# First token pair's FFN steps in two parts, x first in its queue in four parts, four weight blocks decoded ahead of the FFN instead of nine

## The chip, the cores and the metric

The kernel runs on one core of one Trainium2 chip. The metric is the device time of one execution in microseconds (us). The engines are TensorE (PE, its weight loads as PEld), VectorE (DVE), ScalarE (ACT), GpSimd (POOL) and SyncE (SP), which mainly issues DMA transfers. Each engine runs its own instructions in the order in which the program was written down for it.

## The reference

The input x has shape (8, 3008, 256), in fp32. The mixing layer filters each batch along its 3008 positions in the frequency domain, and a feed-forward layer (FFN) with 2048 hidden channels follows:

```python
X = np.fft.rfft(x, axis=1)
Y = X * (filt_r + 1j * filt_i)[None]
y = np.fft.irfft(Y, n=3008, axis=1).astype(np.float32)
t = y.reshape(8 * 3008, 256)
h = t @ w_in                       # 256 -> 2048
g = h * (1.0 / (1.0 + np.exp(-h)))
out = (g @ w_out).astype(np.float32)   # 2048 -> 256
```

The FFN weights `w_in` and `w_out` reach the kernel as 64-bit floats.

## The kernel before

**The transform.** The length 3008 is 47 times 64, and both directions of the transform are matrix products with tables. For a batch the stages are: stage 1 (`pa`, L392 for batch 0, L416 for later ones), a change of layout, `forward` (`pb`, L526), a product with the filter on DVE (`multiply`, L619) and sums (`add`, L627 and L628), `inverse` (`pc`, L660), copies of its result (`rows_first`, L674) that go to DRAM (`d<-q`, L676) and come back in another layout (`load_t4_rows`, L703, to an area of `w_t`), and `stage3` (`pd`, L718), whose result is copied to `y` (L732) as the FFN's operand.

**The head.** Batch 0 is transformed before any FFN work; this stretch is called the head. Its x comes as `x_first` in two transfers of 1536 KB on SP's queue, behind four raw blocks of weights (512 KB each). While PE waits it runs matmuls of no use (`idle`, L1269) on the table `wx_t`. `stage1_first(j)` works on a quarter of the channels each, and DVE transposes its result (L396). The argument `fill` of `forward` sets how many matmuls of no use (L519) stand before it. A later batch's transform is spread over the FFN steps of the batch before it: steps 1 to 6 each take one piece of batch 1's stage 1 (four 512-column matmuls `pa`, L416, and two copies `t<-pa` on ACT, L421).

**The weights.** They come in 16 blocks `j` of raw 64-bit words and are turned into fp32 on the chip. For one block that is: `bits` (two DVE operations, L1170 into `e` and L1172 into `m`), `converted` (two ACT operations on `e`, L1179 and L1180), `added` (DVE, L1186), `signed` (DVE, L1191, needs `converted`), `placed` (DVE, L1198, writes `w_t`). `split` is bits and converted, `rounded` is added and signed. Blocks `2jp` and `2jp+1` hold the weights of the hidden channels of step `jp`, and `combine_weights(jp)` makes three more sums from them (four DVE operations, L948 on `w_t`). The raw words and the intermediate results lie in areas that are free at that time, among them buffers of the pools that the FFN uses later.

**The FFN.** The tokens are in 48 pairs of blocks of up to 256 tokens, six pairs for each batch; each pair takes eight steps (`NJP = 8`), one for each `jp`. A step forms the product of a 2x2 block matrix with seven matrix products instead of eight, in `hidden`, and `project` adds the result through w_out in the same manner one step later (`LAG = 1`). `tokens(pair)` makes the differences of tokens `ty` that `hidden` needs (DVE, L948). In `hidden(step)` (L966) the products go to two PSUM tiles: `px` (A11, then S2, S3 and A22 added on) and `pyz` (A12 in one half, S1 and S4 in the other). Each has one buffer. ACT copies `px` after three of its products (`abc`, L985, L992, L998), DVE adds copies to `pyz` (g0, g2, g1, in this order, L948), ACT applies SiLU (L981), and DVE forms further sums (g4 and g5 in one operation, then g6 and g7). `project(step)` (L1023) makes seven products into four accumulators `acc` (L1044), which stay in PSUM through the eight steps of a pair. After the last step `drain` copies them to a tile `s`, the even ones on ACT and the odd ones on DVE (L1062 and L1064), and POOL makes seven additions on it.

**The order of work.** `hidden` and `project` are generators, and each step has eight rounds. In each round each of the two goes on to its next `yield`; then everything that was put down for that step and round is emitted:

```python
for rnd in range(ROUNDS):
    held = ...
    work = [w for w in work if w in held or next(w, work) is not work]
    until(step + rnd / ROUNDS)
```

`put(step, rnd, piece, *args)` puts a piece of work down, so `(0, 5, (bits, 9), (added, 9))` emits these pieces after round 5 of step 0. In `hidden` g0 is written in round 1, the second copy and the first SiLU in round 2, the third copy and g2 in round 4, and g1 in round 7. The table of decode pieces spreads the blocks that are left after the head over steps 0 to 6. Two more tables, `combines` and `stores`, hold when `tokens(pair)` is emitted and when a pair's result is stored. The head's order is the order of the program's lines.

## Time and profile before

| | |
|---|---|
| median of 3 runs | 2503.47 us (2503.17 to 2504.69) |
| profiled execution | 2503.14 us, its span 2501.4 us |
| granted TensorE clock | 1.00 |
| busy in the span: PE, DVE, ACT, POOL | 2483.7, 1756.4, 1095.6, 430.9 us |
| first product of the FFN begins | 63.06 us |
| pa matmuls of batch 1 in the chain | 71.67, 79.70, 87.74 us |
| PE busy from 63.0 to 111.8 | 48.07 of 48.80 us |
| PE busy from 111.8 to 160.0 | 48.20 of 48.20 us |

Times in the trace count from the span's start. A row of a timeline is: start, duration, engine, line, operation, result and operands with their shapes, number of instructions, and in brackets the idle time before it and what ended that. The mean clock is a share of full speed. The chain of waits is followed back from the last instruction, at each step to what released it.

### The profile page before, as it was taken

How to read it: one execution, taken by the hardware profiler on the slowest of the kernel's cores; microseconds unless marked ns; L12 is line 12 of the kernel's file. 1: busy time of each engine (PE TensorE's matmuls, PEld its weight loads, DVE VectorE, ACT ScalarE, POOL GpSimd, SP SyncE). 2: the span in 40 equal slices, each digit the busy share in tenths (PEclk: the TensorE clock that was granted, in tenths of full speed). 3: DMA queues.
4: the chain of work that ended last, by engine and by line, in shares of the span. 5: the costliest groups of instructions: out<-in, count | busy, mean ns of one | idle time of the engine just before them, and what ended most of it. 6: DMA issues, size and time to landing. Idle time of an engine off the chain costs nothing.

```text
span 2501.4 us, 42281 instructions
## 1 busy us (share of the span) xinstructions
PE 2483.7 (99%) x16242; PEld 2129.1 (85%) x16242; DVE 1756.4 (70%) x3603; ACT 1095.6 (44%) x3006; POOL 430.9 (17%) x673
## 2 busy tenths in 40 slices
PE   8999999999999999999999999999999999999999
PEld 6788888888888888888888888888888888888988
DVE  8866677777777777777777867777677767655544
ACT  4544444444444444444444444444444444444443
POOL 2211112112121122211122112211221111101100
PEclk9999999999999999999999999999999999999999
DMA  8513233213232042420333203321142211200000
GB/s 304 169 60 104 70 72 79 74 38 81 60 93 73 25 93 50 116 63 18 84 74 99 56 26 89 81 68 43 34 107 54 56 43 34 64 21 9 17 9 17
DMA packets 139801, 170.67 MB, mean 68 GB/s; under 512 B 20860, under 2 KB 113372, under 8 KB 138716
## 3 DMA queue, kind: packets, MB, share of 16 engines
q1 hardware_dynamic: 115536, 120.77, 18.2%
q0 software_dynamic: 22080, 44.10, 6.8%
q8 instruction: 127, 2.08, 0.3%
q10 hardware_dynamic: 1984, 3.11, 0.3%
q14 instruction: 74, 0.61, 0.1%
HBM read 96.06 MB, written 81.26 MB: 71 GB/s over the span
## 4 chain that ended last, share of the span: by engine, by line
PE 97%; DMA 1%; DVE 1%; ACT 0%; issue 0%; SPq 0%; POOL 0%; DVEq 0%; ACTq 0%
PE acc L1044 46%; PE px L977 26%; PE pyz L977 20%; PE pd L754 1%; PE pf L486 1%; PE pc L582 1%; PE pb L544 1%; PE pa L392 0%; PE pa L416 0%; DMA w_t<-in_x_first_dram 0%; DMA w_t<-d 0%; DMA d<-q 0%; PE pd L718 0%; PE pb L526 0%; PE pc L640 0%; DVE g L948 0%
## 5 line engine op out<-in xcount | busy, mean ns | idle before, releaser
L1044 PE MATMUL acc<-g,w_t 128*128 128x256 f32 (+1 forms) x5376 | 1507.4, 376 | 3.0 <-ACT o L767 2.5
L1044 PEld LDWEIGHTS acc<-g,w_t 128*128 128x128 f32 x5376 | 1016.2, 190 | 153.8 <-ACT o L767 15.3
L948 DVE TENSOR_TENSOR g<-pyz,abc 128x256 f32<-128x256 f32 (+1 forms) x1152 | 479.7, 416 | 480.3 <-ACT abc L998 240.0
L948 DVE TENSOR_TENSOR g<-g 128x256 f32<-128x256 f32 (+3 forms) x1152 | 589.7, 512 | 196.7 <-ACT g L981 183.6
L977 PE MATMUL px<-ty,w_t 128*128 128x256 f32 (+1 forms) x2304 | 675.6, 375 | 0.6 <-ACT abc L998 0.5
L981 ACT ACTIVATE g<-g 128x256 f32<-128x256 f32 (+1 forms) x1152 | 472.9, 411 | 235.8 <-DVE g L948 235.8
L948 POOL TENSOR_TENSOR s<-s 128x256 f32<-128x256 f32 (+1 forms) x329 | 252.3, 784 | 1419.0 <-DVE s L1062 1093.8
L977 PEld LDWEIGHTS px<-ty,w_t 128*128 128x128 f32 x2304 | 434.1, 190 | 57.2 <-issue 3.7
L977 PE MATMUL pyz<-y,w_t 128*128 128x256 f32 (+1 forms) x1536 | 451.2, 375 | 1.2 <-DVE g L948 1.1
L977 PEld LDWEIGHTS pyz<-y,w_t 128*128 128x128 f32 x1536 | 283.0, 189 | 44.8 <-DVE g L948 5.0
L992 ACT COPY abc<-px 128x256 f32<-128x256 f32 (+1 forms) x384 | 141.4, 368 | 372.7 <-PE px L977 372.7
L981 ACT ACTIVATE g<-px 128x256 f32<-128x256 f32 (+1 forms) x384 | 145.8, 380 | 299.7 <-PE px L977 299.7
L998 ACT COPY abc<-px 128x256 f32<-128x256 f32 (+1 forms) x384 | 141.4, 368 | 308.6 <-PE px L977 308.5
L977 PE MATMUL px<-y,w_t 128*128 128x256 f32 (+1 forms) x768 | 227.4, 378 | 0.1
L977 PE MATMUL pyz<-ty,w_t 128*128 128x256 f32 (+1 forms) x768 | 225.7, 376 | 0.2
L977 PEld LDWEIGHTS px<-y,w_t 128*128 128x128 f32 x768 | 143.4, 189 | 23.7 <-ACT g L981 2.4
L977 PEld LDWEIGHTS pyz<-ty,w_t 128*128 128x128 f32 x768 | 142.0, 190 | 21.9 <-DVE g L948 1.8
L985 ACT COPY abc<-px 128x256 f32<-128x256 f32 (+1 forms) x384 | 135.1, 352 | 34.8 <-PE px L977 34.8
L506 POOL DMA_DIRECT2D d<-tf x96 | 48.5, 506 | 216.3 <-DVE tf L436 210.8
L1062 ACT COPY s<-acc 128x512 f32<-128x512 f32 (+1 forms) x94 | 54.2, 577 | 47.6 <-issue 29.2
L603 POOL DMA_DIRECT2D d<-low x36 | 22.2, 618 | 286.3 <-DVE low L599 286.3
L476 DVE TENSOR_TENSOR uf<-x_all 120x512 f32<-120x512 f32 (+1 forms) x72 | 60.2, 864 | 0.3 <-issue 0.3
(132 smaller groups left out, 1351.5 us busy)
## 6 DMA issues: line engine op xcount, KB each, us to landing
t<-d SPq DMA_DIRECT2D x84, 256.0 KB
t<-d SPq DMA_DIRECT2D x224, 96.0 KB
out_dram<-s SPq DMA_DIRECT2D x64, 256.0 KB
d<-q POOLq DMA_DIRECT2D x48, 256.0 KB, 5.3
x_all<-in_x_dram SPq DMA_DIRECT2D x96, 96.0 KB
x_all<-xr SPq DMA_DIRECT2D x96, 96.0 KB
d<-tf POOLq DMA_DIRECT2D x96, 96.0 KB, 2.7
d<-tq POOLq DMA_DIRECT2D x96, 96.0 KB, 2.9
```

The costliest lines, as they stand in the source:

```text
L476: nc.vector.tensor_tensor(out=out, in0=in0, in1=in1, op=op)
L486: nc.tensor.matmul(out=ps[q][32 * k:32 * k + 32], lhsT=wq_t[rows, k], rhs=rhs[k][rows], start=True, stop=True)
L506: nc.gpsimd.dma_start(out=d1[par, :, grp, at:at + 4], in_=part[rows].rearrange("p q n c -> p (q n) c"))
L544: nc.tensor.matmul(out=ps[k, ri][32 * j:32 * j + 32, a, :], lhsT=dn_t[rows, 4 * (g + a) + at, :], rhs=t2s[g + a][rows, at, :], start=True, ...
L948: eng.tensor_tensor(out=out, in0=in0, in1=in1, op=op)
L977: nc.tensor.matmul(out=out, lhsT=w_t[:, jp, c, 0], rhs=rhs, start=start, stop=True, skip_group_check=True)
L981: nc.scalar.activation(out=g[:, k, 0:n], in_=g[:, k, 0:n] if src is None else src, func=AFT.Silu)
L985: nc.scalar.copy(out=sums[:, 0, 0:n], in_=xo)
L992: nc.scalar.copy(out=sums[:, 1, 0:n], in_=xo)
L998: nc.scalar.copy(out=sums[:, 2, 0:n], in_=xo)
L1044: nc.tensor.matmul(out=acc[pair][i][:, h, 0:n], lhsT=w_t[:, jp, OUT_PLACE.get(c, c), 1], rhs=g[:, k, 0:n], start=(jp == 0 and h == 0), sto ...
L1062: copy(out=s[:, 2 * i:2 * i + 2, 0:n], in_=acc[pair][i][:, :, 0:n])
```

## The change

The steps of pair 0 are done in two parts: its first three (`SPLIT = 3`), then all eight of pair 1, then the other five of pair 0. `drain` therefore runs twice for pair 0, and the second time it adds the accumulators to `s` on DVE. Pair 1's result goes to `x_all`, `tokens(1)` moves from step 7 to step 1, `tokens(2)` from step 11 to step 12 with the tile of `ty[1]`, and the stores of the two pairs change places.

In the head, x comes first in SP's queue, in four transfers of 768 KB, and the raw weights after the tables. The first `idle` runs on a cleared area and so waits for no table; `stage1_first` gets five matmuls of no use before its third and fourth quarter, `forward(0)` gets 12 instead of 8, and the `idle` before stage 3 20 instead of 30.

Before, blocks 0 to 7 were done and 8 nearly done before the FFN. Now blocks 0 to 3 are done, and 4 and 5 as far as `added`. The rest is spread over steps 0 to 9, and raw blocks and intermediate results move to other areas. The diff, cut:

```diff
...
 CH = 256
 STEPS = 2 * len(PAIRS) * NJP
 LAG = 1
+SPLIT = 3
 
 A11, A12, S3, A22, S1, S2, S4 = range(7)
 OUT_PLACE = {A12: S3, S3: A12}
...
 
...
-    return rows.reshape(3, 32, 32, 4, 2, 32).transpose(4, 3, 1, 0, 2, 5)
+    return rows.reshape(3, 32, 32, 4, 4, 16).transpose(4, 3, 1, 0, 2, 5)
 
 
 def laid_out(inputs):
...
 
 
             view = w_t.rearrange("p j c w n -> p (j c w n)")
-            for part in range(2):
-                at = view[:, 3072 * part:3072 * part + 3072]
+            for part in range(4):
+                at = view[:, 1536 * part:1536 * part + 1536]
                 nc.sync.dma_start(out=at, in_=x_first[part].rearrange("q r k n c -> (q r) (k n c)"))
-                xs[part] = at.rearrange("p (k n c) -> p k n c", k=3, c=32)
+                xs[part] = at.rearrange("p (k n c) -> p k n c", k=3, c=16)
...
-        def stage1_first(j):
-
-            ps = [bank(b, f"pa_{b}_{j}_{q}").rearrange("p a c -> p (a c)").rearrange(
-                "p (n c) -> p n c", c=16) for q in range(4)]
-            c0 = 16 * (j % 2)
+        def stage1_first(j, fill=0):
+
+            raw = [bank(b, f"pa_{b}_{j}_{q}") for q in range(4)]
+            ps = [r.rearrange("p a c -> p (a c)").rearrange("p (n c) -> p n c", c=16) for r in raw]
+            for _ in range(fill):
+                nc.tensor.matmul(out=raw[0][:, 0, 0:128], lhsT=wx_t, rhs=wx_t, start=True, stop=True)
             for k in range(3):
                 for q in range(4):
                     rows = slice(32 * q, 32 * q + 32)
-                    nc.tensor.matmul(out=ps[q], lhsT=wx3_t[rows, k], rhs=xs[j // 2][rows, k, :, c0:c0 + 16],
+                    nc.tensor.matmul(out=ps[q], lhsT=wx3_t[rows, k], rhs=xs[j][rows, k],
                                      start=(k == 0), stop=(k == 2), skip_group_check=True)
             for q in range(4):
                 at = 64 * q + 16 * j
...
 
                 view = w_t.rearrange("p j c w n -> p (j c w n)")
                 room = {2: view[:, 1792:3840], 3: view[:, 3840:5888],
-                        5: raws["first"].bitcast(FP32)}[g].rearrange("p (k i r c) -> p k i r c", k=2, i=2, r=2)
+                        5: view[:, 6144:8192]}[g].rearrange("p (k i r c) -> p k i r c", k=2, i=2, r=2)
                 z, pt = room[:, k, 0], room[:, k, 1]
             else:
                 z = zpool.tile([128, 2, C], FP32, name=f"z_{b}_{g}_{k}", tag="z")
...
 
     pairs = token_pairs()
     n_steps = len(pairs) * NJP
+    steps = [divmod(step, NJP) for step in range(n_steps)]
+    steps = [*steps[0:SPLIT], *steps[NJP:2 * NJP], *steps[SPLIT:NJP], *steps[2 * NJP:]]
     v, gp = nc.vector, nc.gpsimd
     ty, g_t, acc, unfinished = {}, {}, {}, []
 
...
     def tokens(pair):
 
...
-        t = typool.tile([128, 4, CH], FP32, name=f"ty_{pair}", tag="ty")
+        t = ty[1] if pair == 2 else typool.tile([128, 4, CH], FP32, name=f"ty_{pair}", tag="ty")
...
-        pair, jp = divmod(step, NJP)
+        pair, jp = steps[step]
...
-        pair, jp = divmod(step, NJP)
+        pair, jp = steps[step]
         n, g = pairs[pair][3], g_t.pop(step)
-        if jp == 0:
+        new = step == 0 or steps[step - 1][0] != pair
+        if new:
             acc[pair] = {}
-        last = jp == NJP - 1
+        last = step == n_steps - 1 or steps[step + 1][0] != pair
 
         order = PROJECT
-        if jp == 0 and step in joined:
+        if new and step in joined:
             order = PROJECT[0:2] + PROJECT[3:5] + PROJECT[2:3] + PROJECT[5:]
             if step in turned:
                 order = order[1::-1] + order[2:]
-        elif jp == 0:
+        elif new:
             order = PROJECT[2:3] + PROJECT[0:2] + PROJECT[3:]
...
-                             start=(jp == 0 and h == 0), stop=last, skip_group_check=True)
+                             start=(new and h == 0), stop=last, skip_group_check=True)
...
-    results = {}
+    results, parts = {}, set()
 
     def drain(pair, i):
         n = pairs[pair][3]
-
-        if i == 0:
+        more = pair == 0 and i in parts
+        if pair == 1:
+            results[pair] = x_all.rearrange("p i a n -> p (i a n)").rearrange("p (k n) -> p k n", n=CH)
+        elif i == 0 and not more:
             results[pair] = spool.tile([128, 8, CH], FP32, name=f"s_{pair}", tag="s")
         s = results[pair]
         copy = v.tensor_copy if i % 2 else nc.scalar.copy
         if i < 3:
-            copy(out=s[:, 2 * i:2 * i + 2, 0:n], in_=acc[pair][i][:, :, 0:n])
+            dst, src = s[:, 2 * i:2 * i + 2, 0:n], acc[pair][i][:, :, 0:n]
+        else:
+            dst, src = s[:, 6, 0:n], acc.pop(pair)[3][:, 0, 0:n]
+        if more:
+            combine(v, dst, src, dst, ALU.add)
+        else:
+            copy(out=dst, in_=src)
+        if pair == 0 and not more:
+            parts.add(i)
             return
-        copy(out=s[:, 6, 0:n], in_=acc.pop(pair)[3][:, 0, 0:n])
+        if i < 3:
+            return
...
-            if j in (6, 7):
-
-                room = w_t.rearrange("p j c w n -> p (j c w n)")[:, (7168, 13056)[j - 6]:][:, 0:1024].bitcast(U32)
-                e, m = room[:, 0:512], room[:, 512:1024]
-            elif j in (0, 1, 4, 5):
+            if j in (0, 1):
                 if "scratch" not in raws:
                     raws["scratch"] = gpool.tile([128, 4, 512], U32, name="scratch", tag="g")
                 e, m = (raws["scratch"][:, 2 * (j % 2) + i] for i in range(2))
...
                 m = ppool.tile([128, 512], U32, name=f"m_{j}", tag="p")
             lo, hi = words[:, :, 0], words[:, :, 1]
             ef, mf = e.bitcast(FP32), m.bitcast(FP32)
-            ends = (lo, hi) if j in (2, 3, 6, 7) else (m, e)
+            ends = (lo, hi) if j in (2, 3, 4, 5) else (m, e)
             raws[j] = lo, hi, e, m, ef, ends[0].bitcast(FP32), ends[1].bitcast(FP32), ends[1]
...
-    def idle(n, ps=None):
-
-        ps = (ps or bank(0, "idle")).rearrange("p a c -> p (a c)")
+    def idle(n, operand=None):
+
+        ps = bank(0, "idle").rearrange("p a c -> p (a c)")
+        rows = wx_t if operand is None else operand
         for _ in range(n):
-            nc.tensor.matmul(out=ps[:, 0:128], lhsT=wx_t, rhs=wx_t, start=True, stop=True)
+            nc.tensor.matmul(out=ps[:, 0:128], lhsT=rows, rhs=rows, start=True, stop=True)
 
...
-    idle(18)
+    blank = x_all[0:96, 0, 0, 0:128]
+    v.memset(blank, 0.0)
+    idle(14, operand=blank)
 
     part, second = spectral(0), spectral(1)
-    weights(0, 1, 2, 3)
     part["load_first"]()
     nc.sync.dma_start(out=d_t[:, 0:16], in_=d_dram[:, 0:16])
     nc.sync.dma_start(out=f_all[:, :, 0:4], in_=filt_a)
...
     nc.sync.dma_start(out=d_t[:, 16:NS], in_=d_dram[:, 16:NS])
     nc.sync.dma_start(out=e_t[:, 2:NG], in_=e_dram[:, 2:NG])
     nc.sync.dma_start(out=wi_t, in_=ws_dram.ap())
-    weights(4, 5, 6, 7)
-    for pair in ((0, 1), (2, 3)):
-        split(*pair)
-        rounded(*pair)
+    weights(0, 1, 2, 3)
 
...
     for j in range(4):
-        part["stage1_first"](j)
+        part["stage1_first"](j, 5 * (j > 1))
     second["load_two"]()
-    weights(8)
-    part["forward"](0, fill=8)
-    placed(0, 1)
+    weights(4, 5)
+    part["forward"](0, fill=12)
     for g in range(1, 4):
         part["forward"](g)
 
...
     for k in range(2):
         part["add"](NG - 1, k)
     part["load_t4_rows"](0)
-    bits(4)
+    bits(0, 1)
     inverse(4)
-    bits(5)
     inverse(5)
-    combine_weights(0)
-    bits(6, 7, 8)
+    converted(0, 1)
+    added(0, 1)
     part["load_t4_rows"](1)
     part["load_t4_rows"](2)
-    converted(4, 5)
-    placed(2, 3)
-    weights(9)
+    bits(2, 3)
+    converted(2, 3)
+    signed(0, 1)
+    placed(0, 1)
     for u in range(2):
         second["stage1"](u, False)
-    converted(6, 7)
-    converted(8)
-    rounded(4, 5)
-    placed(4, 5)
-    rounded(6, 7)
-    placed(6, 7)
-    added(8)
-    signed(8)
-    idle(30)
+    combine_weights(0)
+    rounded(2, 3)
+    placed(2, 3)
+    combine_weights(1)
+    bits(4, 5)
+    converted(4, 5)
+    added(4, 5)
+    idle(20)
     for g in range(4):
         part["stage3"](g)
     gp.tensor_copy(out=gate, in_=y[0, 0][:, 0, 28:29])
...
     idle_wide(1)
     nc.sync.dma_start(out=wi_t, in_=wi_dram.ap())
     second["load_x"](2)
-    weights(10, 11, 12)
+    weights(6, 7)
     second["load_x"](3)
     early[0] = None
     plan_rest(0, part)
     for g in (4, 5):
-        put(7, 0, part["load_t4"], g)
+        put(8, 0, part["load_t4"], g)
     for step, t, dram in ((20, wq_t, wq_dram), (40, dn_flat, dn_dram),
                           (40, en_flat, en_dram), (30, wm_t, wm_dram)):
         put(step, 0, lambda t=t, dram=dram: nc.sync.dma_start(out=t, in_=dram.ap()))
     for b in range(1, B):
         plan(b, second if b == 1 else spectral(b))
     for step, rnd, *todo in (
-            (0, 1, (combine_weights, 1)), (0, 5, (bits, 9), (added, 9)),
-            (1, 0, (converted, 9)), (1, 1, (placed, 8), (signed, 9), (bits, 10)),
-            (1, 2, (weights, 13)), (1, 5, (combine_weights, 2), (converted, 10)),
-            (2, 1, (placed, 9), (added, 10), (signed, 10), (placed, 10), (bits, 11)),
-            (2, 2, (weights, 14, 15)), (2, 5, (combine_weights, 3), (converted, 11)),
-            (3, 1, (combine_weights, 4), (added, 11), (signed, 11), (bits, 12)),
-            (3, 5, (placed, 11), (converted, 12)),
-            (4, 1, (combine_weights, 5), (added, 12), (signed, 12), (placed, 12)),
-            (4, 5, (bits, 13), (added, 13)), (5, 0, (converted, 13)),
-            (5, 1, (bits, 14), (added, 14), (signed, 13), (placed, 13)),
-            (5, 5, (combine_weights, 6), (converted, 14)), (5, 7, (bits, 15)), (6, 0, (converted, 15)),
-            (6, 1, (signed, 14), (placed, 14), (added, 15), (signed, 15), (placed, 15)),
-            (6, 5, (combine_weights, 7))):
+            (0, 1, (signed, 4), (placed, 4), (signed, 5)), (0, 5, (placed, 5), (bits, 6), (added, 6)),
+            (1, 0, (converted, 6), (weights, 8, 9, 10)), (1, 1, (combine_weights, 2)), (1, 5, (signed, 6), (placed, 6)),
+            (2, 1, (bits, 7), (added, 7)), (2, 2, (converted, 7), (weights, 11)),
+            (2, 5, (bits, 8), (signed, 7), (placed, 7)), (3, 0, (converted, 8)),
+            (3, 1, (added, 8), (signed, 8), (placed, 8)), (3, 2, (weights, 12)), (3, 5, (bits, 9), (added, 9)),
+            (4, 0, (converted, 9)), (4, 1, (bits, 10), (signed, 9), (placed, 9)),
+            (4, 2, (converted, 10), (weights, 13)), (4, 5, (added, 10), (signed, 10), (placed, 10)),
+            (5, 1, (combine_weights, 3), (bits, 11)), (5, 2, (converted, 11), (weights, 14, 15)),
+            (5, 5, (added, 11), (signed, 11), (placed, 11)),
+            (6, 1, (combine_weights, 4), (bits, 12)), (6, 2, (converted, 12)),
+            (6, 5, (added, 12), (signed, 12), (placed, 12)),
+            (7, 1, (combine_weights, 5), (bits, 13)), (7, 2, (converted, 13)),
+            (7, 5, (added, 13), (signed, 13), (placed, 13)),
+            (8, 1, (combine_weights, 6), (bits, 14)), (8, 2, (converted, 14)),
+            (8, 5, (added, 14), (signed, 14), (placed, 14), (bits, 15)), (9, 0, (converted, 15)),
+            (9, 1, (added, 15), (signed, 15), (placed, 15)), (9, 5, (combine_weights, 7))):
         for piece, *args in todo:
             put(step, rnd, piece, *args)
 
...
     stores = (((10, 1), (10, 5)), ((19, 1), (23, 5)), ((31, 1), (31, 5)), ((35, 1), (35, 5)),
               ((43, 1), (43, 5)), ((50, 1), (51, 1)))
     for pair in range(len(pairs)):
-        step, rnd = combines[pair % per] if pair != 1 else (7, 5)
+        step, rnd = combines[pair % per] if pair not in (1, 2) else ((1, 5), (12, 5))[pair - 1]
         pending.append((pair // per * STEPS + step + rnd / ROUNDS, 98, lambda pair=pair: tokens(pair)))
         for chunk in range(2 if pair < len(pairs) - 1 else 0):
-            step, rnd = stores[pair % per][chunk]
+            step, rnd = stores[pair % per][chunk] if pair > 1 else (stores[1 - pair][chunk] if pair == 0 else (13, 1 + 4 * chunk))
             pending.append((pair // per * STEPS + step + rnd / ROUNDS, 99 + chunk,
                             lambda pair=pair, chunk=chunk: output(pair, chunk)))
     pending.sort(key=lambda p: p[:2])
```

More of the change, by code (lines that the diff above doesn't have):

```diff
@@ L1127, in load_weights @@
     def load_weights(j, queue=None):
-        if j in (8, 11, 12, 13):
-            pool, tag = (t4pool, "t4") if j in (11, 12) else (upool, "u")
+        if j in (6, 7, 8, 11, 12, 13):
+            pool, tag = (upool, "u") if j in (6, 11) else (t4pool, "t4")
             raw = pool.tile([128, 2, 512], U32, name=f"raw_{j}", tag=tag)
@@ L1138, in load_weights @@
                 raws["y"] = raws["at"]
-                raws.setdefault("first", raws["at"])
             elif j == 4:
                 raws["at"] = spool.tile([128, 2048], U32, name=f"raw_{j}", tag="s")
-            elif j == 6:
-                raws["at"] = gpool.tile([128, 2048], U32, name=f"raw_{j}", tag="g")
             elif j in (9, 14):
                 raws["at"] = raws["y"]
-            at = 1024 * (j in (1, 3, 5, 7, 10, 15))
+            at = 1024 * (j in (1, 3, 5, 10, 15))
             raw = raws["at"][:, at:at + 1024].rearrange("p (w n) -> p w n", w=2)
```

## The prediction

> **What bounds the kernel now.** I read the page first: busy times and the chain that ended last.
>
> ```profile
> span 2501.4 us, 42281 instructions
> PE 2483.7 (99%) x16242; PEld 2129.1 (85%) x16242; DVE 1756.4 (70%) x3603; ACT 1095.6 (44%) x3006; POOL 430.9 (17%) x673
> PE 97%; DMA 1%; DVE 1%; ACT 0%; issue 0%; SPq 0%; POOL 0%; DVEq 0%; ACTq 0%
> ```
>
> TensorE is busy 99% of the span. The change removes no matrix product, so it can gain only where PE waits, and that is the head before the first FFN product. It can lose wherever a new wait stops PE. The chain of waits, in order of time (start, duration, piece), shows the head:
>
> ```profile
> 2.77 9.77 DMA w_t<-in_x_first_dram
> 12.67 10.59 PE pa L392 x95
> 23.89 1.88 DVE w_t L396 x3
> 25.81 1.26 PE pb L526 x29
> ...
> 36.20 0.59 ACT q L674
> ...
> 37.81 4.82 DMA d<-q
> 42.76 4.41 DMA w_t<-d
> 47.24 4.02 DMA d<-q
> ...
> 51.91 5.15 DMA w_t<-d
> 57.20 4.01 PE pd L718 x251
> ...
> 62.36 0.56 DVE y L732
> 63.01 0.70 DVE ty L948
> ```
>
> x holds PE until 12.67, two round trips through DRAM follow, and the FFN starts at 63.06 (first L977 row). In the windows PE is busy 48.07 of the 48.80 us from 63.0 to 111.8, and in the chain the pa matmuls of steps 1 to 6 stand 8.03 apart (71.67, 79.70, 87.74). So the FFN's opening has next to nothing to win.
>
> Third, the timelines of VectorE and ScalarE there, for what one weight block costs and how the sums g stand to it:
>
> ```profile
> 107.98 0.42 DVE L948 TENSOR_TENSOR g<-pyz,abc 128x256 f32<-128x256 f32 x1
> 108.89 0.69 DVE L948 TENSOR_TENSOR g<-g 128x512 f32<-128x512 f32 x1 [0.48 <-ACT g L981]
> 109.49 0.42 DVE L1170 TENSOR_SCALAR e<-raw 128x512 uint32<-128x512 uint32 x1
> ...
> 110.16 0.42 DVE L948 TENSOR_TENSOR g<-pyz,abc 128x256 f32<-128x256 f32 x1
> 110.50 0.88 DVE L948 TENSOR_TENSOR g<-g 128x256 f32<-128x256 f32 x2
> ```
>
> ```profile
> 109.95 0.72 ACT L1179 ACTIVATE e<-e,bias_t 128x512 f32<-128x512 uint32 x1 [0.84 <-DVE e L1170]
> 110.70 0.72 ACT L1180 ACTIVATE e<-e,bias_t 128x512 uint32<-128x512 f32 x1
> 111.33 0.35 ACT L992 COPY abc<-px 128x256 f32<-128x256 f32 x1
> ```
>
> A block costs DVE bits 0.67 (two at 0.335 start to start), added, signed and placed 0.60 each, together 2.48; ACT 1.38 (109.95 to 111.33); a combine of a pair of blocks costs DVE 1.47. The last ACT rows matter most: the conversion waits for DVE's bits, and the next copy of px waits for the conversion.
>
> **The head, part by part.** Quarter 1 of x is 0.79 MB, first on its queue, beside 0.24 MB of small tables. Before, 1.07 MB had moved at 5.0 us (sum of the DMA rows by microsecond), so it lands near 5.5 and stage 1 starts near 5.6, 7.1 earlier. The other quarters follow 1.9 us apart at the 410 GB/s shown; 24 matmuls take 2.65 (10.59/4), so they hold nothing. Against that: five fillers twice, ten instructions each at 0.114 (60 idle matmuls took 6.86), +2.3; a slow first part, as the first microsecond of stage 1 made 8 matmuls and the next 16, +0.45; fill 12 instead of 8, 24 instructions at 0.128 (16 took 2.05), 3.1. Stage 1 ends at 5.6+10.6+2.3+0.45 = 18.9 and pb starts at 22.0 instead of 25.81: **3.8 earlier**. The transposes (16 at 0.64, following each quarter) end near 21.4, inside the fill. Raw blocks 0 to 3 now come behind the tables: the same bytes in another order, landed by about 27, long before their bits.
>
> What follows shifts by 3.8 up to the inverse: DVE's copy of q ended at 46.35, now 42.55. There the changed list puts decode work that before lay under the wait for x. DVE must do, in order: added(0,1) 1.21, bits(2,3) 1.34, signed(0,1) 1.20 (0.5 later, since ACT's conversions stand behind its DMA issue, which at 47.24 waited for a row load to land), placed 1.21, combine 1.47, added and signed(2,3) 2.41, placed 1.21, combine 1.47, first bits of block 4 0.42: 12.4, so 55.0. Then comes the wait that I hold decisive here: ACT converts blocks 4 and 5, 2.85, ahead of its six copies of y (L732). So y starts at 57.9, although PE's stage 3, which ended at 61.2, could end at 56.7: 3.8 earlier, and 0.7 because raw_9 no longer moves beside the last row load (5.15 against the 4.41 of the one before). The copies take 2.86 (2.39 for five, 0.47 for one): FFN at 60.7, **a gain of 2.3** (bounds: 0.5, if the hold of 0.5 on ACT grows to the 2.3 by which its issue at 47.24 lay behind its copy at 44.90; 5.3, if only transfers and PE bind: 3.8, 0.7, and the 0.80 marked issue at 61.20).
>
> **The FFN's first ten steps.** Before, 7 blocks were left for seven steps; now 10 whole blocks, and the second halves of 4 and 5. pyz is one buffer: the next step's first product of it waits until g1 has read it, so I count from g1 to g1. Fixed part: g1 to the sum of two (g4:5) 0.91 (107.98 to 108.89), that sum 0.60, g0 0.34, g6 and g7 0.79. Work put after g0 delays g2, and work after g2 delays g1; without either, g2 and g1 stand 1.76 apart (132.66, 134.42), so 1.42 behind g2 is free; and some 0.25 to 0.35 of slack before pyz absorbs more (g1 ended at 108.40, pyz came at 108.82). By step, work behind g2 less 1.42 and that slack: step 0, placed, bits, added 1.87, +0.2, and 0.4 since 1.82 ahead of g2 (signed, placed, signed) replaces a combine of 1.47; step 1, tokens(1) 1.52 (63.01 to 64.54) and signed, placed 1.2, +1.0; step 2, bits, signed, placed 1.87, +0.2; step 3, two drain copies 0.97 and bits, added 1.27, +0.6; step 4, added, signed, placed 1.82, +0.15.
> Steps 5 and 6: ACT's order has converted(11) and (12) ahead of the t copies and of abc3 (L998), which g2 and the A22 product need, and DVE gives the bits only after a combine. 0.91+0.60+0.34+0.79+1.47+0.42 = 4.53 to the bits, 0.03 and 1.38 for the conversion, 0.96 two t copies (2.02 for four), 0.4 abc3, 0.34 g2, 1.82 added, signed, placed: 9.5 to g1, +1.5 each.
> Steps 7 and 8 have no pa matmuls, so PE needs only 6.03 (fourteen at 0.43): 9.5-0.96 = 8.5, +2.5; step 8 has bits(15) too, +3.2. Step 9, +0.3.
> Sum 11.55, taken as **12**, as a late step leaves the next no slack before pyz. Bounds: 5.4 if ACT never holds abc3 (DVE alone makes 6.94 in steps 5 to 7, below the 8.03 of 5 and 6, and 7.6 in step 8: 0.9 and 1.6 instead of 8.7), 13 if the slack is nowhere there.
>
> The rest costs nothing by rows: pair 0's second drain, four adds from PSUM (0.61, three at 512 columns, and 0.36) instead of two copies each on DVE and ACT, falls in a step without decode, where DVE waits 0.95 and 1.33 (132.66, 134.42) beside g; uncovered it costs up to 1. POOL's adds at 0.784 keep their number and POOL is busy 17%. tokens(2) writes into ty[1] after pair 1's last step, so it waits for nothing. The later weight DMAs (512 KB, 1.25 us at 410 GB/s) are issued a step ahead of their bits, while DMA is 61% busy.
>
> Net -2.3+12 = +9.7 on the profiled 2503.14 (span 2501.4 and 1.74 outside it); the median 2503.47 stands 0.33 above: 2513.2, rounded down to **2513.0**.
>
> **Rivals.** (A) Not slower. Transfers alone set the head (-5.3), and ACT never holds abc3, so steps 5 to 8 cost DVE's part alone: -5.3+5.4, 2503.6. It decides if abc3 is never later than DVE's own list. For it: ACT is 44% busy. Against: its in-order row at 109.95 waits for bits, and here nothing stands between those and abc3. 0.12.
> (B) A clock gate. PE idles from 56.7 to 60.7 before the FFN. After the 1.1 us of idling before stage 1 its first microsecond ran at half rate (8 against 16). Half rate through the first step's fourteen matmuls of 0.43 costs up to 3.0 and one microsecond of it 0.5; I take 1.7: 2514.7. 0.10. The granted clock reads 1.00 in all windows, which speaks against it.
> [...]
> (C) The change doesn't do what it says: x is early, but the table wx3 on the other queue, which landed by 7.37, is what stage 1 then waits for; 1.8 of the gain goes, 2514.8. For it: both share the engines. Against: it is 192 KB and issued first. 0.12.
> (D) Faster: as A, and DVE's pieces fit the idle time so that the FFN pays under 0.3 and the head keeps 5.3: 2498.4. 0.04, since steps 7 and 8 alone hold more DVE work (2.4 of sums, 1.47, 2.48 = 6.4) than PE has (6.03).
> The forecast has 0.62.
>
> **How the numbers follow.** About 0.2%, 5.0 us, is what a measurement of this kernel can tell from no change. The forecast's own bounds are -5.3 to -0.5 and 5.4 to 13: 2503.6 to 2516. The range leaves out A and D (0.16) and reaches past B and C with a microsecond of an uncovered drain and a step more: 2506 to 2518. Slower by over 0.2%, above 2508.5: B, C and nearly all of the forecast, 0.82; same: A and a little of the forecast, 0.14; faster 0.04.
>
> **What would show it.** In the profile after: pa L392 from 5.6; pb L526 at 22; the first y copy near 58 behind the ACT conversions of blocks 4 and 5; FFN from 60.7; g1 to g1 of 9.5 in steps 5 and 6 and over 8 in 7 and 8, with "ACT abc" as the releaser before g2; DVE at nine tenths over the first ten steps. I am wrong if the pa groups stay 8.03 apart, or if FFN starts before 58.

## The result and the profile after

The changed kernel takes 2519.07 us (median of 6 runs, 2517.83 to 2520.27) against 2503.74 us of the kernel before (6 runs, 2502.51 to 2504.69). The ratio is 1.0061, with a 95% interval of 1.0048 to 1.0074. It is slower by 15.3 us. The forecast was slower by 9.7 us, and its range ended 1.07 us below the measured median. One profiled execution of the study, that of e11_tokens (4793.61 us at a granted clock of 0.79, against 2500.06 to 2503.51 us in its kernel's other runs), is left out everywhere below.

The profiled execution took 2519.81 us, 16.7 more than that of before. In the changed code most lines stand two to five numbers later: L977 is now L981, L998 is L1002, L948 is L952, L1044 is L1049, L1179 and L1180 are L1188 and L1189. The first lines of the page:

```profile
span 2518.0 us, 42288 instructions
PE 2491.2 (99%) x16242; PEld 2128.8 (85%) x16242; DVE 1759.4 (70%) x3608; ACT 1096.6 (44%) x3006; POOL 431.5 (17%) x673
PE 96%; DVE 3%; ACT 1%; DMA 0%; issue 0%; POOL 0%; DVEq 0%
```

PE has as many matmuls as before and is busy 7.5 us longer; DVE is busy 3.0 us longer and ACT 1.0. What grew most is the share of the chain that lies on DVE and ACT: 4% of the span, where it was 1%. So the loss is made of waits, and of matmuls that ran slowly. The chain of waits in the head (start, duration, piece):

```profile
1.29 7.24 DMA wx<-wx_tbl
8.67 8.37 PE pa L394 x48
...
25.24 2.88 PE pb L521 x24
28.12 1.18 PE pb L528 x32
...
58.90 0.44 DVE w_t L952
...
60.82 0.74 ACT e L1188
...
63.67 2.24 ACT y L734 x6
65.96 1.22 PE px L981 x2
```

Stage 1 waits for the table wx3 (`wx`) and no longer for x, whose first quarter had landed by 5.34 us, when SP's queue went on behind it. Its first half takes 8.37 us. Its weight loads show the pace, one row for each four matmuls:

```profile
13.07 0.38 PEld L394 LDWEIGHTS pa<-w_t,wx 32*128 32x128 f32 x4 [0.47 <-issue]
13.92 0.38 PEld L394 LDWEIGHTS pa<-w_t,wx 32*128 32x128 f32 x4 [0.47 <-issue]
...
15.15 0.21 PEld L394 LDWEIGHTS pa<-w_t,wx 32*128 32x128 f32 x4 [0.22 <-issue]
15.58 0.21 PEld L394 LDWEIGHTS pa<-w_t,wx 32*128 32x128 f32 x4 [0.22 <-issue]
```

The groups start 0.85 us apart until 14.7 us and 0.43 apart behind that, so PE ran at half pace until then. The granted clock reads 1.00 in all of these windows, so that column does not show this stretch.

The first FFN product comes at 65.96 us, which is 2.9 us later than before instead of 2.3 us earlier. The rows ahead of it, ACT's conversions and its copies of y, are the wait that the prediction called decisive.

Behind that, the four-product groups of `acc`, one for each step from step 1 on, give the pitch of the steps. They begin at 78.14, 87.31, 95.63, 104.29, 112.54, 122.10, 129.95, 138.54 and 147.80 us; before, at 73.66, 81.69, 89.73, 97.76, 105.52, 113.76, 119.95, 126.02 and 132.06. ACT's timeline in the step that takes 9.56 us:

```profile
111.77 0.72 ACT L1188 ACTIVATE e<-e,bias_t 128x512 f32<-128x512 uint32 x1 [1.79 <-DVE e L1179]
112.53 0.72 ACT L1189 ACTIVATE e<-e,bias_t 128x512 uint32<-128x512 f32 x1
113.16 1.05 ACT L423 COPY t<-pa 128x512 f32<-128x512 f32 x2
114.10 0.38 ACT L1002 COPY abc<-px 128x256 f32<-128x256 f32 x1
```

ACT stands idle for 1.79 us until DVE has the bits of the block, and the copy of px, for which PE and the sum g2 wait, stands behind the conversion and two more copies.

From the first FFN product to the last of these groups it takes 81.84 us, and 69.00 before: 12.8 us. The head adds 2.9 us. Another 1.7 us go by the first `pc` rows of the next batch (198.80 us, 181.35 before), and the rest of the trace gives 0.85 us back, in small steps of up to 0.4 us over the later batches.

### The profile page after: what moved, and what is told of

It is laid out like the page before. It is cut to its first block, busy times and chain, and to the rows that moved or that the text cites. A ratio compares the mean times of both kernels' runs of the same rounds, so it can differ in the third digit from the quotient of the medians.

```text
span 2518.0 us, 42288 instructions
## 1 busy us (share of the span) xinstructions
PE 2491.2 (99%) x16242; PEld 2128.8 (85%) x16242; DVE 1759.4 (70%) x3608; ACT 1096.6 (44%) x3006; POOL 431.5 (17%) x673
## 4 chain that ended last, share of the span: by engine, by line
PE 96%; DVE 3%; ACT 1%; DMA 0%; issue 0%; POOL 0%; DVEq 0%
PE acc L1049 45%; PE px L981 25%; PE pyz L981 19%; PE pd L756 1%; PE pf L488 1%; PE pc L584 1%; PE pb L546 1%; DVE g L952 1%; PE pa L394 1%; PE pc L662 0%; PE pb L528 0%; PE pa L418 0%; DVE w_t L1207 0%; DMA wx<-wx_tbl 0%; DVE w_t L952 0%
## 5 line engine op out<-in xcount | busy, mean ns | idle before, releaser
L1049 PE MATMUL acc<-g,w_t 128*128 128x256 f32 (+1 forms) x5376 | 1507.7, 376 | 3.0 <-ACT o L769 2.5
L1049 PEld LDWEIGHTS acc<-g,w_t 128*128 128x128 f32 x5376 | 1016.1, 190 | 154.4 <-ACT o L769 15.3
L952 DVE TENSOR_TENSOR g<-pyz,abc 128x256 f32<-128x256 f32 (+1 forms) x1152 | 479.7, 416 | 483.7 <-ACT abc L1002 246.8
L952 DVE TENSOR_TENSOR g<-g 128x256 f32<-128x256 f32 (+3 forms) x1152 | 590.7, 513 | 196.8 <-ACT g L985 183.6
L981 PE MATMUL px<-ty,w_t 128*128 128x256 f32 (+1 forms) x2304 | 676.5, 375 | 5.8 <-ACT abc L1002 5.8
L981 PEld LDWEIGHTS px<-ty,w_t 128*128 128x128 f32 x2304 | 434.1, 190 | 63.8 <-ACT abc L1002 7.8
L952 POOL TENSOR_TENSOR s<-s 128x256 f32<-128x256 f32 (+1 forms) x322 | 246.8, 784 | 1389.1 <-DVE s L1075 1046.6
L981 PE MATMUL pyz<-y,w_t 128*128 128x256 f32 (+1 forms) x1536 | 452.7, 376 | 6.8 <-DVE g L952 6.6
L981 PEld LDWEIGHTS pyz<-y,w_t 128*128 128x128 f32 x1536 | 282.7, 189 | 53.8 <-DVE g L952 14.5
L1002 ACT COPY abc<-px 128x256 f32<-128x256 f32 (+1 forms) x384 | 141.7, 369 | 306.2 <-PE px L981 306.1
L981 PE MATMUL px<-y,w_t 128*128 128x256 f32 (+1 forms) x768 | 227.5, 378 | 0.9 <-ACT y L734 0.9
L981 PE MATMUL pyz<-ty,w_t 128*128 128x256 f32 (+1 forms) x768 | 225.7, 376 | 0.0
L981 PEld LDWEIGHTS px<-y,w_t 128*128 128x128 f32 x768 | 143.9, 190 | 22.9 <-DVE q L777 1.9
L981 PEld LDWEIGHTS pyz<-ty,w_t 128*128 128x128 f32 x768 | 142.4, 190 | 20.8 <-DVE g L952 0.5
```

Of the source, the lines that this page charges most:

```text
L952: eng.tensor_tensor(out=out, in0=in0, in1=in1, op=op)
L981: nc.tensor.matmul(out=out, lhsT=w_t[:, jp, c, 0], rhs=rhs, start=start, stop=True, skip_group_check=True)
L1002: nc.scalar.copy(out=sums[:, 2, 0:n], in_=xo)
L1049: nc.tensor.matmul(out=acc[pair][i][:, h, 0:n], lhsT=w_t[:, jp, OUT_PLACE.get(c, c), 1], rhs=g[:, k, 0:n], start=(new and h == 0), stop=la ...
```

## Experiments

All are edits of the changed kernel, and "the changed kernel" below has 2519.07 us. The diffs are against it, cut, unless another kernel is named. The kernel before ran beside each group, at 2503.4 to 2503.9 us.

**The late table, the idle operand, the place of the conversions.** Four kernels on one chip.

```diff
-    nc.scalar.dma_start(out=wx3_t, in_=wx3_dram.ap())
+    nc.sync.dma_start(out=wx3_t, in_=wx3_dram.ap())
```

> The changed kernel, with the 192-KB table wx3 issued ahead of x on SP's queue instead of on ACT's. Theory (stage 1 waited for wx3, not for x): wx3 lands near 3.5, x's first quarter near 6, and stage 1 starts when the idle matmuls end at 7.4 instead of 8.67: the head is 1.2 us shorter, about 2518. Rival (x itself is that late, and the release put down to wx3 is only the last of two): stage 1 stays at 8.6 or later, and the time at 2519.

Measured: 2515.72 us (ratio to before 1.0047, 1.0033 to 1.0060). Stage 1 starts at 7.42 us, directly behind the idle matmuls, and pb at 25.5 instead of 28.1. So wx3 was what it waited for, and the first quarter of x was there by then. The profiled run, which had the slowest time of this kernel's runs (2518.84 us), shows 2.6 us less in the head, 1.25 by the earlier start and as much by a faster first half of stage 1 (7.12 us). It lost 1.4 of them again at the start of the FFN: the first step took 7.1 us, at a granted clock of 0.50 from 65 to 70 us. The median fell by 3.35 us where the theory had 1.2; what the other 2 us are was not found.

```diff
-    v.memset(blank, 0.0)
+    v.memset(blank, 1.0)
```

> The changed kernel, with the area that the first idle matmuls read set to 1.0 instead of 0.0. Theory (matmuls on zeros do not bring TensorE up to speed): the last idle matmuls run at 0.11 us instead of 0.226, the first 48 matmuls of stage 1 take 5.5 us instead of 8.37, pb starts 3 us earlier, and the time is about 2516. Rival (the pause of 1.25 us before stage 1, or the time since the start, sets it, whatever the operands): 48 matmuls in 8.4 us again, 2519.

Measured: 2518.07 us (1.0060, 1.0047 to 1.0073). The 28 idle matmuls took 5.40 us instead of 6.34, and stage 1's first half 7.13 instead of 8.37, though PE now paused 2.16 us before it. PE reached full pace at 5.4 us, and behind the pause the granted clock read 0.59 from 8 to 12 us. On this run alone the theory looked right in part; the later runs below take it back.

```diff
-            (5, 1, (combine_weights, 3), (bits, 11)), (5, 2, (converted, 11), (weights, 14, 15)),
+            (5, 1, (combine_weights, 3), (bits, 11)), (5, 2, (weights, 14, 15)), (5, 4, (converted, 11)),
...
-            (6, 1, (combine_weights, 4), (bits, 12)), (6, 2, (converted, 12)),
+            (6, 1, (combine_weights, 4), (bits, 12)), (6, 4, (converted, 12)),
```

Steps 7 and 8 are edited in the same way.

> The changed kernel, with the conversions of blocks 11 to 14 put down after round 4 instead of round 2 of steps 5 to 8, so behind the copy abc of L1002 on ACT. Theory (in these steps the conversion holds abc, and with it g2): g2 comes without its wait, but signed now waits for the later conversion: g1 to g1 of 8.9 in steps 5 and 6 (9.56 now), 7.6 in step 7 (8.59), 8.2 in step 8 (9.26), 3 us in all, 2516. Rival (DVE's own list alone binds these steps): no change of the pitch, 2519.

Measured: 2515.73 us (1.0046, 1.0034 to 1.0059). ACT's timeline in the same step:

```profile
110.45 0.38 ACT L1002 COPY abc<-px 128x256 f32<-128x256 f32 x1
110.71 0.74 ACT L1188 ACTIVATE e<-e,bias_t 128x512 f32<-128x512 uint32 x1
```

The copy now comes first, and the wait of 1.79 us is gone. The pitch of the four steps fell from 9.56, 7.85, 8.59 and 9.26 us to 8.69, 6.97, 7.40 and 8.07, together 4.1 us. The conversions did hold `abc`. What is left over 8.24, 6.19, 6.07 and 6.04 before is 4.6 us.

> The three edits together: wx3 first, ones in the idle area, the four conversions behind abc. By the theories: stage 1 starts at 7.0 and at full speed (pb 4.5 us earlier), the steps 5 to 8 give back 3 us: about 2511.5. By the rivals: 2519. If only the first FFN products stay slow (granted clock 0.83 in the window from 60 to 70 us), about 1 us of the changed kernel's loss remains in both.

Measured: 2511.55 us (1.0033, 1.0020 to 1.0045), with pb at 23.6 us and the FFN at 61.49. The median is a tenth of a microsecond from the sum of the theories. Part of that is luck: the five runs lie between 2509.66 and 2515.39 us, and stage 1's first half took 5.43 us here, but 7.47 and 7.24 in e6_head and e7_pool below, which have the same ones in the idle area and no pause before stage 1 either.

**Is it the order or the amount?** The next kernel keeps the split, the head and every piece, and only puts the pieces of steps 0 to 9 elsewhere, for example:

```diff
-            (5, 1, (combine_weights, 3), (bits, 11)), (5, 2, (converted, 11), (weights, 14, 15)),
-            (5, 5, (added, 11), (signed, 11), (placed, 11)),
+            (3, 3, (bits, 10)), (4, 0, (combine_weights, 3), (added, 10), (converted, 9)), (4, 1, (converted, 10)),
...
+            (5, 0, (bits, 11)), (5, 1, (converted, 11), (bits, 12), (added, 11)),
+            (5, 2, (signed, 11), (weights, 14, 15)), (5, 3, (combine_weights, 4)), (5, 5, (added, 12)),
```

> The changed kernel with another table of decode pieces for steps 0 to 9: the same pieces, the same split of pair 0, but bits, added, signed and placed put down in rounds 0 to 4 or at a step's end where DVE waits, and no conversion between a step's products and the copy that its sums need. Theory (the loss of steps 0 to 9 is one of order, not of DVE's sum of work): from the first FFN product to the four-product group of step 9 it takes as long as before, 11 to 12 us less than in the changed kernel: 2507. Rival (ten blocks are simply too much work for DVE, whose own part is 6.4 of 6.03 us in steps 7 and 8): at most the 4 us that moving the conversions gave, 2515.

Measured: 2507.82 us (1.0017, 1.0008 to 1.0026). The same work costs 11.3 us less. The last groups stand 8.08, 6.04, 6.04 and 6.04 us apart, which is what PE alone needs (fourteen products at 0.43; the first of them has four of `pa` too). So DVE had room for ten blocks; it was the order that cost. Not all of it came back with this table: in the profile, from the first FFN product to the group of step 9, it takes 72.15 us, 9.7 less than in the changed kernel and still 3.1 more than before. 0.7 us of that goes by the first group, and two of the steps behind it lost 0.9 and 1.5 us. PE's timeline shows why, in the second of them:

```profile
101.21 0.70 PE L981 MATMUL pyz<-ty,w_t 128*128 128x256 f32 x2 [1.50 <-DVE g L952]
```

This is S1's product, and it waits for g0: both use the one tile `pyz`, though not the same half. My table had put a combine and `added` ahead of g0 in that step. The prediction had counted pyz's wait for g1 only.

**The head.** e6_head has the table of e5_table, wx3 first, ones in the idle area, tokens(2) in step 11, and ACT's conversions of blocks 4 and 5 behind the copies of y. In e7_pool, POOL also does the combines of jp 0 and 1. The conversions' new place:

```diff
-    converted(4, 5)
...
     for g in range(4):
         part["stage3"](g)
+    converted(4, 5)
```

> As e5_table, with wx3 first and ones in the idle area, with the conversions of blocks 4 and 5 behind the copies of y on ACT, and with tokens(2) in step 11 again. Theory (in the head ACT's conversions hold y, DVE's list the rest): the first FFN product comes at 59 instead of 65.96, no loss in steps 0 to 12: 2503.5-4-1 = 2498.5, and 1 to 2 us more if PE falls to half speed before the FFN. Rival (the transfers of d bind the head and the conversions are only put off, to hold abc in step 0): first product at 61.5, 2502.

> As e6_head, with the combines of jp 0 and 1 in the head on POOL instead of DVE. Theory (DVE's list of decode pieces sets when y can be copied): its list is 2.9 us shorter, the first FFN product at 57 to 57.5, 2497. Rival (transfers, or POOL's four additions at 0.78 each, set it): no earlier than in e6_head, or step 1 waits for w_t by 1 us.

Measured: 2507.95 and 2507.63 us (1.0017 and 1.0015), no better than e5_table at 2507.82. The first FFN product came at 62.48 and 63.40 us, so earlier than in e5_table (66.52), but then:

```profile
65.19 0.70 PE L981 MATMUL px<-ty,w_t 128*128 128x256 f32 x2 [1.61 <-ACT abc L989]
```

The conversions were only put off, as the rival said, and now held the first copy of px. In addition, bits(6) waited until 70.0 us for its raw block, whose transfer was issued between two loads of x. My theories for the head fell here, with a forecast of 59 and of 57 us for that product. Putting the conversions behind y only moves their wait; the next kernels have them ahead of it.

**A better order in the head.** e8_best loads both wx tables ahead of x and raw block 6 early, converts blocks 4 and 5 before DVE signs and places blocks 2 and 3, and has a table in which nothing stands ahead of g0:

```diff
-    combine_weights(0)
-    rounded(2, 3)
-    placed(2, 3)
-    combine_weights(1)
+    combine_weights(0, None, gp)
+    added(2, 3)
     bits(4, 5)
     converted(4, 5)
+    signed(2, 3)
+    placed(2, 3)
+    combine_weights(1, None, gp)
     added(4, 5)
-    idle(20)
+    idle(28)
```

> The changed kernel with: both tables wx ahead of x on SP's queue; nine first idle matmuls on the table wx_t, not 14 on a cleared area; raw block 6 loaded with 4 and 5; in the head added(2,3), bits and conversions of 4 and 5 ahead of signed and placed(2,3), so that ACT converts them before y is there; combines of jp 0 and 1 on POOL; 28 idle matmuls before stage 3; tokens(2) in step 11; and a table of decode pieces in which no piece stands between a product and the sum g0 that S1's tile waits for. Theory (order, the late table and the clock are all of the loss): stage 1 from 7.4, pb at 24 to 25, first FFN product at 60 to 60.5 (63.06 before), steps 0 to 12 as long as before: 2500 to 2501. Rival (the pieces are too much for DVE even in a good order, or the y copies come no earlier): 2504 or more.

> As e8_best, with 20 instead of 28 idle matmuls before stage 3. Theory (PE's pause before stage 3 halves its clock, there and in the first FFN products): stage 3's matmuls or the first FFN step at half speed, a granted clock below 1 between 52 and 68 us, 1 to 2 us slower than e8_best. Rival (the pause does not matter): the same time and a clock of 1.00.

> As e8_best, with the changed kernel's 14 first idle matmuls on the cleared area. Theory (matmuls on constant data do not bring TensorE up to speed): stage 1's first 48 matmuls take 7 us or more, against 5.5 to 6.5 in e8_best, and pb comes 1 us later. Rival (any matmul counts): the longer idle brings PE up earlier, 48 matmuls in 5.5 us, pb no later than in e8_best.

Measured: 2502.47, 2502.02 and 2502.49 us, ratios 0.9996 (0.9987 to 1.0005), 0.9994 and 0.9994 (both 0.9985 to 1.0003). The whole loss is gone with the split kept. The time from the first FFN product to the group of step 9 is 68.2 us in e8_best, 69.00 before. The head gained less than I expected: the first FFN product came at 62.58 us in e8_best and 60.48 in e10_zeros, against 60 to 60.5 expected and 63.06 before.

The two questions about the clock came out against me. With 20 idle matmuls stage 3 took 6.53 us instead of 5.54, at a granted clock of 0.50 from 56 to 60 us; but with 28 the clock was 0.68 there in e8_best and 1.00 in e10_zeros, and the medians do not differ. And on the cleared area, which I had held to be no work for TensorE, PE came up to speed during the idle matmuls, and stage 1's first half took 5.43 us. Their rows in the changed kernel, e2_idle_ones and e10_zeros:

```profile
1.08 6.34 PE L1279 MATMUL idle<-x_all 96*128 96x128 f32 x28 [1.08 <-DVE x_all L1290]
```

```profile
1.08 5.40 PE L1279 MATMUL idle<-x_all 96*128 96x128 f32 x28 [1.08 <-DVE x_all L1290]
```

```profile
1.08 5.91 PE L1279 MATMUL idle<-x_all 96*128 96x128 f32 x28 [1.08 <-DVE x_all L1290]
```

Zeros took 6.34 us in four of the profiles, 5.91 here and 5.16 in e12_no_pool below; ones took 5.40, 6.15 in e4_all_three, and 6.34 in e6_head and e7_pool. So the operand alone does not decide.

POOL's part showed a price of its own. While POOL made the combine of jp 0 in e8_best, DVE's bits rose from 0.42 to 0.96 us:

```profile
50.38 4.00 POOL L952 TENSOR_TENSOR w_t<-w_t 128x256 f32<-128x256 f32 x4 [9.35 <-DVE w_t L1207]
```

```profile
51.96 0.96 DVE L1179 TENSOR_SCALAR e<-raw 128x512 uint32<-128x512 uint32 x1
52.84 0.96 DVE L1181 TENSOR_SCALAR m<-raw 128x512 uint32<-128x512 uint32 x1
```

In these rows both engines took longer than elsewhere: POOL's four additions 1.00 us each, where the mean over the trace before is 0.78 (0.69 to 1.23), and three of DVE's four `bits` 0.95 to 0.96 us, where all four take 0.42 in e12_no_pool below, without POOL's additions beside them. Why, and which of the two waits for which, is not shown.

**The last two.** Both keep the 14 idle matmuls on the cleared area. The diff is e11_tokens against e10_zeros; e12_no_pool has `combine_weights(1)` on DVE as well:

```diff
-    combine_weights(0, None, gp)
+    combine_weights(0)
...
-        step, rnd = combines[pair % per] if pair not in (1, 2) else ((1, 5), (11, 5))[pair - 1]
+        step, rnd = combines[pair % per] if pair not in (1, 2) else ((1, 5), (11, 1))[pair - 1]
```

> As e10_zeros, with the combine of jp 0 on DVE again (on POOL it ran beside DVE's bits, whose rows rose from 0.42 to 0.96 us) and with tokens(2) after round 1 of step 11 instead of round 5, ahead of g2 and away from pair 1's drain. Theory: PE no longer waits 1.0 us for g at the end of step 11 (1.5 us with what follows), bits at 0.42 again: 2500.5, faster than before with an interval below 1. Rival: tokens(2) delays g2 there as it delayed g1, and DVE's list in the head is 1.47 longer: 2502.5.

> As e11_tokens, with the combine of jp 1 on DVE too, so POOL does no decode work. Theory: this one runs beside no bits but beside added(4,5) on DVE; moved to DVE it puts 1.47 into the list ahead of DVE's copies of y, the FFN starts up to 1 us later: 2501.5. Rival (the shared time of DVE and POOL costs as much as it saves): the same as e11_tokens.

Measured: 2501.65 us (0.9992, 0.9983 to 1.0001) and 2501.22 us (0.9990, 0.9981 to 0.9999). e12_no_pool shows tokens(2) at its new place without a wait of PE behind it: g1 to g1 there is 6.04 us, and 7.89 in e6_head to e10_zeros. Its FFN starts at 61.57 us, 1.5 earlier than before. Taking the last combine off POOL cost nothing. e12_no_pool has the lowest median of the study, 2.5 us or 0.10% under the kernel before and 17.9 us under the changed one. It is a small gain, with an interval that ends just below 1, and the two kernels here cannot be told apart: e11_tokens has runs from 2500.06 to 2503.51 us, e12_no_pool from 2500.22 to 2502.59.

## Why the prediction was wrong, and where it was right

**Right: the sign, the mechanism and the sum of the FFN's steps.** Forecast 11.55, taken as 12. Of the 12.84 us measured, 1.0 is the slow clock of the first step (5.72 us from first product to second step's, 4.72 before), which leaves 11.8. Step by step, forecast and measured (from the groups above): step 0 +0.6 and +0.6 without the clock; step 1 +1.0 and +1.1; step 2 +0.2 and +0.3; step 3 +0.6 and +0.6; step 4 +0.15 and +0.5; steps 5 and 6 +1.5 each and +1.3, +1.7; step 7 +2.5 and +2.5; step 8 +3.2 and +3.2. (Step 9's +0.3 lies behind the last group.) From g1 to g1 it takes 9.56, 9.56, 8.59 and 9.26 us in steps 5 to 8, and the prediction's working gives 9.5, 9.5, 8.5 and 9.2. e3_convert_late shows ACT's place for the conversion (4.1 us), and e5_table and e8_best show that the rest goes with the order of the pieces too. Rival A is out. One sign did not come: DVE was busy 61.95 of the 82 us from 66 to 148, three quarters and not nine tenths; in steps 5 and 6 it waited 2.44 us for ACT's `abc` each time.

**Right: the lengths in the head.** From pb to DVE's copy of q it takes 19.9 us in both traces. The decode list from there to block 4's first bits took 12.2 us, forecast 12.4; the conversions 2.8 (2.85); copies of y and the first product 2.4 (2.86).

**Wrong: "stage 1 starts near 5.6".** The step that failed is the one that let x's first quarter alone decide. x itself was where the working had it: its first quarter had landed by 5.34 us, forecast 5.5. The table wx3 goes through another queue; it was issued 0.55 us after x, not first as I wrote against rival C, and landed at 8.53 us. This is rival C. I had given it 0.12 and 1.8 us; it cost 3.1. The 7.37 us of its price was a bound from a trace with smaller blocks in front. By the landing times in the traces transfers of the two queues landed in turn: before, the raw block issued first had landed at 4.40, `wx_t` at 4.57, the second raw block at 6.00 and wx3 at 6.77 us; in the changed kernel x's first quarter at 5.33, `wx_t` at 5.52, x's second quarter at 7.64 and wx3 at 8.53. So in both traces wx3 came behind the second transfer of SP's queue, and that had grown from a raw block of 512 KB to a quarter of x of 768 KB. e1_wx3_first, which issues wx3 ahead of x on SP's queue, takes the wait away; it does not tell whether the queue or the place in it did so.

**Wrong: the size of the slow stretch in stage 1.** The +0.45 should have been 2.9: the first 48 matmuls took 8.37 us, and 5.43 at full pace in e10_zeros. From 8.67 to 25.24 stage 1 took 16.6 us, and the sum without this term was 12.9; of these 3.7 us the other 0.7 are the fillers (2.6 for 2.3) and the matmuls' full pace (11.0 for 10.6). With 3.1 for the table and 3.2 here beyond the 0.45, less 0.2 of the idle matmuls behind, pb stood at 28.1 instead of 22.0. The shift of 5.3 us from 60.7 to 65.96 follows from these alone, less 0.8 by which the later pieces were shorter. The size is partly luck: e3_convert_late, with the same head, took 6.85 us for the first 48 matmuls.

The reading behind the 0.45 was wrong too. The 8 matmuls of the first microsecond and 16 of the next are counts of those that touch a window; stage 1 of the kernel before ran at full pace from its second group on, 0.43 us from group to group:

```profile
13.18 0.23 PEld L392 LDWEIGHTS pa<-w_t,wx 32*128 32x128 f32 x4 [0.20 <-issue]
13.61 0.23 PEld L392 LDWEIGHTS pa<-w_t,wx 32*128 32x128 f32 x4 [0.20 <-issue]
```

The half pace of that trace lies elsewhere, in its first idle matmuls: they start 0.21 us apart from 4.62 to 10.3 us and 0.11 apart behind that. So PE needed 5.7 us from its first matmul to full pace there, which the prediction did not see, and 13.6 in the changed kernel. The granted clock of 1.00, which I held against rival B, reads the same in that half-paced stretch. Before, that time lay under the wait for x; with x and the table there early, stage 1 itself runs in it.

**Wrong: rivals counted as if only one could happen.** B, the clock before the FFN, came true as well in this execution: 1.0 us instead of 1.7, at a granted clock of 0.50 from 66 to 68 us. It is not in every execution: the first step takes 4.78 us in e2_idle_ones and 4.77 in e3_convert_late, which have the same order of work in the head, and 5.72 here. The pause of 4.0 us that rival B rests on did not come: PE's longest before the FFN was 1.45 us, with the small matmuls of stage 3 between the pauses. The clock fell all the same. No run shows the 1.7, which was my choice between the estimates 0.5 and 3.0. Nor do the runs show one length for the stretch at half pace after a start: in e6_head PE kept it, without a pause, through 6.3 us of idle matmuls and about 4 us of stage 1 (an estimate: twice the 2.04 us that its first 48 matmuls, at 7.47 us, took beyond 5.43). B and C add to the forecast, and a range that reached to each of them alone could not hold their sum.

**Missed: tokens(2).** It "waits for nothing", as I wrote, but work waits for it. In step 12 it stands between two products with the filter and g1:

```profile
174.18 0.70 PE L981 MATMUL pyz<-y,w_t 128*128 128x256 f32 x2 [0.88 <-DVE g L952]
```

This is most of the last 1.15 us of the 1.7; the other 0.55 had gone by the `pd` rows at 164.93 us (148.63 before), with step 9 in it. I had checked the operands of the moved piece and not its new neighbours.

The sum: 5.3 for the head, 1.4 for the FFN's first steps and their clock (12.84 and 0.55 against 12), 1.15 with tokens(2), less the 0.85 that the rest of the trace gives back, is 7.0. The profiled execution was 7.0 above its forecast of 2512.8. What the small steps of the 0.85 are stays open.

**Still open:** what decides when TensorE reaches full speed. Over the thirteen profiles used here it came between 4 us (e12_no_pool) and 13.6 us (the changed kernel) after the first matmul, with zeros, ones and the table as operands, with and without a pause before stage 1. Open too is what lowers the granted clock around stage 3 and the FFN's start, where it read between 0.50 and 0.69 in a window of 2 to 4 us in nine of these profiles: in e2_idle_ones it read 0.57 from 56 to 60 us, behind pauses of 0.58 and 0.70 us, and in e3_convert_late it stayed at 1.00 through pauses of 0.65, 1.19 and 1.60. The runs of the changed kernel differ by 2.4 us, which both together could move; that they do is not shown.

## What to carry to other kernels

When work is moved behind the start of a loop, count each engine's queue in order, piece by piece, from one hand-over to the next. DVE had room for the work that was moved; its order cost 11 to 12 us, and another order with the same work cost nothing. When a large transfer is pulled to the front, list everything else that its consumer reads, and find for each table what now moves ahead of it or beside it. Rivals that do not exclude each other belong in the forecast with their expected price, and into the range as a sum.

## What the runs showed of the hardware that I had not expected

A half-speed stretch of TensorE cost up to 2.9 us, beside the 4.1 of four badly placed conversions: 48 matmuls of stage 1 took 5.43 us in three profiles and up to 8.37 in others. In the changed kernel the granted clock read 1.00 all the while, and only the distance from matmul to matmul shows it (0.85 us for four, 0.43 later). A table of 192 KB on its own queue landed in both traces only behind the second transfer of another queue, at 6.77 us behind blocks of 512 KB and at 8.53 behind quarters of 768 KB. And DVE's `bits`, beside POOL's additions in e8_best, took 0.96 us instead of 0.42.
